# Feature products of q as 64x32 tiles, and output stores placed behind feature moves, in a fused attention and feed-forward kernel

## The chip, the core and the metric

The kernel runs on one NeuronCore of a Trainium2 chip. The core has a matrix engine (TensorE, "PE" in the profile, its weight loads "PEld"), a vector engine (VectorE, DVE), a scalar engine (ScalarE, ACT), a general engine (GpSimd, POOL) and a queue that issues transfers (SyncE, SP). They run side by side and wait for each other through semaphores. The metric is the device time of one execution in microseconds; the lower the better.

## The reference

Inputs are q, k and v of 4 batches, 4 heads, 1088 positions and 32 channels, two sketch matrices S1 and S2 of 8x32, and the two weight matrices of a feed-forward layer, 128x2048 and 2048x128. All are 32-bit floats.

```python
def phi(x):                       # 64 features of each position
    a = einsum('rd,bhsd->bhsr', S1, x)
    b = einsum('rd,bhsd->bhsr', S2, x)
    return einsum('bhsi,bhsj->bhsij', a, b).reshape(..., 64)
kv  = einsum('bhsf,bhsd->bhfd', phi(k), v)
z   = sum(phi(k), axis=2)
num = einsum('bhsf,bhfd->bhsd', phi(q), kv)
den = einsum('bhsf,bhf->bhs', phi(q), z)[..., None] + 1e-6
x   = (num / den).transpose(0, 2, 1, 3).reshape(4352, 128)
h   = maximum(x @ w_in, 0)
out = (h * h) @ w_out
```

## The kernel before

The feed-forward layer is most of the work. The 4352 rows of x are cut into 12 chunks: 4 batches with 3 chunks each, of 384, 384 and 320 positions. For each chunk the 2048 hidden units are cut into 16 blocks of 128. One block of one chunk is a step, and there are 192 steps, in the list `steps`. In step i TensorE makes the first product of step i+3 (`ffn1`, L908, output `pg`, half-precision operands) and the second product of step i (`ffn2`, L939, output `po`, 32-bit operands, collected over the 16 blocks). In between the relu and the square of `pg` are made by ScalarE, VectorE or GpSimd (L902, L918, L920, L929); `balance()` chooses which.

The attention of later chunks is made in the same steps, a little in each. A planner, `_Plan`, keeps a list of functions for each step. `P.add` puts a function at the first step that lies behind what it needs and where its engine has room, and `P.fix` puts it at a given step. In the end the main loop emits, for each step, the two products and then the functions in that step's list, in the order in which they were put in. Each engine works off its own instructions in the order of emission, and so does the SP queue, which stands still while the transfer at its head waits for its data.

For a chunk of batches 1 to 3 the attention goes through these functions:

- `a_qT` turns q (VectorE), and `a_qgy` (L564) multiplies it with `sw`, which holds the folded sketch matrices. The contraction runs over 64 rows, in two halves r, and the positions of the chunk are two halves of 192 (160 in the last chunk). Its output is the tile `qg`, named `qk` in the profile; half r goes to bank r of it.
- `a_tq` (L573) turns the outcome back, `a_den` makes the denominators, `a_qp2` (GpSimd) the 64 features, and `a_bk` (L612) turns these again, into `ft` and `u1`.
- `a_mv` (L626) moves rows of features between partitions, by transfers on the SP queue: two copies inside `ft` and then four from `u1`, named `u` in the profile, to `ft`. Two of the four overwrite what the first two read, and so they wait for these.
- `a_nd2` (L637) multiplies the features with `kw`, which comes from k and v; its output `ndn` is the attention before scaling. It is a product of 64 rows by 32 columns in eight tiles of the array.

`x_group` emits on TensorE, in this order: `a_nd2` of one chunk, `a_qgy` of the next chunk, and, where a new batch is due, `a_kf2` (L431), the features of k, again as 64 by 32 tiles. In batch 0 `a_ndn` (L550) stands in the place of `a_nd2`, with the same tile shape. One group has `a_qgy` alone, the first of batch 1. A matmul of 32-bit floats shows as two instructions in the trace.

The output of a chunk is scaled (`f_sc`, L985), turned (`f_sT`, L994, tile `oT` of two buffers) and stored by four transfers on the SP queue (`out_dma`, L1010). For chunk m these stand at steps 16(m+1) and 16(m+1)+2. The loads of k, v and q for the next batch (`loads`, L131, L141) are on the same SP queue.

Of the kernel before, what the change touches and what calls it, by code (L numbers as in the profile page):

```python
# [15 lines left out]
def _ap(t: bass.AP, p0: int, np_: int, off: int, free):  # L16

    p = list(t.ap)[0]
    return bass.AP(
        t.tensor, t.offset + p0 * p[0] + off, [[p[0], np_]] + [list(d) for d in free]  # L20
    )
# [52 lines left out]
def kernel(  # L74
# [13 lines left out]
    B, H, S, D = 4, 4, 1088, 32  # L88
# [9 lines left out]
    SP = 128 * NT  # L98
# [140 lines left out]
    st = {}  # L239
# [3 lines left out]
    sw = [cpool.tile([128, 64], F32, name="sw%d" % i) for i in range(2)]  # L243
# [265 lines left out]
    def width(ch):  # L509
        return min(192, (S - 384 * ch) // 2)  # L510
# [46 lines left out]
    def a_qgy(b, ch, qg):  # L557

        n = width(ch)
        st[b, "qg", ch] = qg  # L560
        for r in range(2):
            for g in range(2):
                c0 = 384 * ch + n * g
                nc.tensor.matmul(  # L564
                    qg[64 * g : 64 * g + 64, 512 * r : 512 * r + n],
                    sw[b % 2][64 * r : 64 * r + 64, :],
                    qT[64 * r : 64 * r + 64, c0 : c0 + n],
                )

# [421 lines left out]
    def f_sT(b, ch):  # L991
        n = min(384, S - 384 * ch)
        oT = fpool.tile([128, 384], F32, tag="oT", bufs=2, name="oT")
        nc.vector.transpose(oT[:, 0:n], st["sc", b, ch][:, 0:n])  # L994
        out_dma(b, ch, oT, n)

    def f_ob(b, ch):
        n = min(384, S - 384 * ch)
# [9 lines left out]
    def out_dma(b, ch, ob, n):  # L1008
        for dm in range(4):
            nc.sync.dma_start(  # L1010
                bass.AP(
                    out.tensor, out.offset + (b * S + 12 * ch) * 128 + 32 * dm,
                    [[G * 128, 32], [128, n // 32], [1, 32]],
                ),
                _ap(ob, 32 * dm, 32, 0, [[32, n // 32], [1, 32]]),
            )
# [106 lines left out]
    for h in range(H):  # L1123
        c0 = 12 * (h % 2)
# [38 lines left out]
    P = _Plan(NS + 4, {"PE": 0.95, "DVE": 1.2, "ACT": 0.6, "POOL": 5.0, "SP": 9.0})  # L1163
    for m in range(B * 3 - 1):
        b, ch = divmod(m, 3)
# [26 lines left out]
    def old_chunk():  # L1192

        b, ch = 0, 1
        P.at["qb", b, ch] = -1
        for e in range(E):
            P.add(("qa", b, ch, e), "DVE", 0.58, [("qb", b, ch)], a_qa, b, ch, e)
            P.add(("qp", b, ch, e), "DVE", 0.56, [("qa", b, ch, e)], a_qp, b, ch, e)
        P.add(("nd", b, ch), "PE", 0.9, [("qp", b, ch, 1)], a_nd, b, ch)
        P.add(("x1", b, ch), "DVE", 0.9, [("nd", b, ch)], a_x1, b, ch)  # L1200
        P.add(("x2", b, ch), "DVE", 0.9, [("x1", b, ch)], a_x2, b, ch)
        P.add(("x3", b, ch), "DVE", 0.7, [("x2", b, ch)], a_x3, b, ch)
        P.at["N"] = P.at["x3", b, ch]
        P.add(("xd", b, ch), "SP", 0.0, [("x3", b, ch)], a_xd, b, ch)
        ready(b, ch)

    def feature_tasks(b, ch):
        need = [("qg", b, ch)] if ("qg", b, ch) in P.at else []
        if b == 0:
            for s_ in range(2):  # L1210
                for i in range(2):
                    P.add(("sh", b, ch, s_, i), "DVE", 0.58, need, a_sh, b, ch, s_, i)
                P.add(("qpn", b, ch, s_), "POOL", 0.95, [("sh", b, ch, s_, 1)], a_qpn, b, ch, s_)
            P.at["X"] = P.at["sh", b, ch, 1, 1]
            return
        P.add(("tq", b, ch), "DVE", 0.5, need, a_tq, b, ch)
        P.at["X"] = P.at["tq", b, ch]
        P.add(("den", b, ch), "DVE", 1.1, [("tq", b, ch)], a_den, b, ch, lag=0)
        for e in range(2):
            P.add(("qp2", b, ch, e), "POOL", 1.05, [("den", b, ch)], a_qp2, b, ch, e)  # L1220
        for e in range(2):
            P.add(("bk", b, ch, e), "DVE", 0.5, [("qp2", b, ch, e)], a_bk, b, ch, e)
            P.add(("mv", b, ch, e), "SP", 0.0, [("bk", b, ch, e)], a_mv, b, ch, e)
        P.at["mv", b, ch, 1] += 5

    def run(*todo):
# [17 lines left out]
    def nd_tasks(b, ch):  # L1244

        need = ["N", ("kw", b)]
        need += [("qpn", b, ch, 1)] if b == 0 else [("mv", b, ch, 1)]
        qc, kb = None, None
        time = 0.75 if b == 0 else 0.4
        if b > 0 and (b, ch) != (B - 1, 2):  # L1250
            qc = divmod(3 * b + ch + 1, 3)
            need += ["X", ("qT", *qc), ("sy", qc[0])]
            time += 0.45
        if (b == 0 and ch == 2) or (ch == 0 and 0 < b < B - 1):
            kb = b + 1
            need += ["X"] + [("kT", kb, x_) for x_ in range(3)]
            time += 0.5
        P.add(("nd", b, ch), "PE", time, need, x_group, b, ch, qc, kb)
        if qc:
            P.at["qg", *qc] = P.at["nd", b, ch]  # L1260
        if kb:
            P.at["kf", kb] = P.at["nd", b, ch]

    def x_tasks(b, ch):
        if b == 0:
            P.add(("dT", b, ch), "DVE", 0.58, [("nd", b, ch)], a_dT, b, ch)
            P.add(("rd", b, ch), "DVE", 0.4, [("dT", b, ch)], a_rd, b, ch, lag=0)
            P.add(("rb", b, ch), "DVE", 0.58, [("rd", b, ch)], a_rb, b, ch, lag=0)
            P.add(("x", b, ch), "DVE", 0.56, [("rb", b, ch)], a_x, b, ch, lag=0)
        else:  # L1270
            P.at["x", b, ch] = P.at["nd", b, ch]
        P.add(("ax", b, ch), "ACT", 0.5, [("x", b, ch)], a_ax, b, ch)
        P.add(("sum", b, ch), "PE", 0.17, [("ax", b, ch)], a_sum, b, ch)
        P.add(("rs", b, ch), "DVE", 0.53, [("sum", b, ch)], a_rs, b, ch)
        if b > 0:
            P.add(("xs", b, ch), "DVE", 0.56, [("rs", b, ch)], a_xs, b, ch, lag=0)
        P.add(("s2", b, ch), "DVE", 0.53, [("sum", b, ch)], a_s2, b, ch)
        if b == 0:
            P.add(("xs", b, ch), "POOL", 0.95, [("rs", b, ch)], a_xs, b, ch)
            P.at["N"] = P.at["s2", b, ch]  # L1280
        else:
            P.at["N"] = max(P.at["s2", b, ch], P.at["xs", b, ch])
        P.add(("bt", b, ch), "POOL", 1.0, [("s2", b, ch)], a_beta, b, ch)
        if (b, ch) == (B - 1, 2):
            P.add(("bcol", b, ch), "DVE", 0.5, [("bt", b, ch)], a_bcol, b, ch, lag=3)
        ready(b, ch)
# [14 lines left out]
    def turn_q(n, i):  # L1301
        c0, c1 = 384 * i, min(384 * i + 384, S)
        P.add(("qT", n, i), "DVE", 0.55, [("qg", n, i - 1)] if i else [("qg", n - 1, 2)] if n > 1 else [],
              a_qT, n, c0, c1, first=48 * (n - 1) + 14, slow=1.2)

    def kv_tasks(n):
        P.add(("kv", n), "PE", 1.3, [("kp", n, 0), ("kp", n, 1), "N"], a_kv9, n)
        P.add(("kvs", n), "ACT", 0.3, [("kv", n)], a_kvs, n)
        P.add(("gm", n), "DVE", 0.2, [("kv", n)], a_gm, n)
        P.add(("kvT", n), "PE", 0.3, [("kvs", n), ("gm", n)], a_kvT, n)  # L1310
        P.add(("kw", n), "ACT", 0.3, [("kvT", n)], a_kw, n, lag=1)
        P.add(("sy", n), "DVE", 0.2, [("kvT", n)], a_sy, n, lag=1)
        P.at["N"] = max(P.at["kw", n], P.at["sy", n])

    def turn_k(n):
        s0 = 48 * (n - 1) - (n > 1) * 16
        for i in range(5):
            at = 2 * i if n == 1 else s0 - 16 if i == 0 else s0 + 1 + 2 * i
            P.fix(("ld", n, i), "SP", 0.0, at, loads, n, i)
        for part in range(3):  # L1320
            P.add(("kT", n, part), "DVE", (0.71, 0.71, 0.2)[part], [], a_kT, n, part,
                  first=max(s0, 6), slow=n > 1 and 1.2)

    P.at["X"] = P.at["N"] = -1
    P.add(("kw", 0), "ACT", 0.4, [], a_kw, 0)
    old_chunk()
    f_br(0, 0, 0, 1)
# [18 lines left out]
    for m in range(3, 3 * B):  # L1346
        n, ch = divmod(m, 3)
        if m == 99:
            P.cap["DVE"] = CAP
        if ch == 0 and n + 1 < B:  # L1350
            turn_k(n + 1)
        nd_tasks(n, ch)
        if True:
            x_tasks(n, ch)
        if m + 1 < 3 * B:
            feature_tasks(*divmod(m + 1, 3))
        if False:
            x_tasks(n, ch)
        if ch == 0 and n + 1 < B:
            k_tasks(n + 1)  # L1360
        if ch == 1 and n + 1 < B:
            kv_tasks(n + 1)
        if m + 2 < 3 * B:
            turn_q(*divmod(m + 2, 3))

    def balance():

# [85 lines left out]
```

## Time and profile before

| | |
|---|---|
| median of four runs | 195.74 us (195.16 to 196.02) |
| the profiled execution: its own time | 196.02 us |
| its span in the trace | 194.2 us |
| busy, TensorE matmul | 186.7 us (96%) |
| busy, ScalarE | 130.6 us (67%) |
| busy, VectorE | 118.6 us (61%) |
| busy, GpSimd | 90.5 us (47%) |
| share of 16 DMA engines used by the main queue | 28.7% |
| mean granted clock of TensorE | 0.988 |

The span runs from the first to the last instruction of the traced execution; the execution's own time also holds what lies around it. Busy time of TensorE is modelled to the end of each matmul, and neighbouring matmuls overlap, so a group's cost is read from its start to the start of what follows. "64*32" in a row is the shape of the tile in the array, rows by columns, and "64x192" the operand that streams through it.

### The profile page before, as it was taken

The numbers are of one execution on the slowest core, as the hardware profiler recorded it, in microseconds if no ns is written. First come the engines' busy times: TensorE is split into PE (matmuls) and PEld (weight loads), VectorE is DVE, ScalarE is ACT, GpSimd is POOL, SyncE is SP. The second block draws the span as 40 slices with busy tenths as digits, with TensorE's granted clock in tenths as the row PEclk, the third lists the DMA queues.
The fourth block names the chain that finished last, engine by engine and source line by source line (L and its number), as shares of the span: only waits on it lengthen the run. The fifth ranks groups of instructions, "written<-read, shape, count | busy, mean of one in ns | idle before, by whom it ended". The sixth has DMA issues, their size and how long they took to land.

```text
span 194.2 us, 4289 instructions
## 1 busy us (share of the span) xinstructions
PE 186.7 (96%) x1468; PEld 109.3 (56%) x1468; DVE 118.6 (61%) x284; ACT 130.6 (67%) x322; POOL 90.5 (47%) x172
## 2 busy tenths in 40 slices
PE   7997999999999999999999999999999999999990
PEld 2663565565546546655556556555565555556990
DVE  3958875975639946367339855585381834637750
ACT  3325676956949958678659776577594966856840
POOL 5835553783444944325646941533666542251000
PEclk9999699999999999999999999999999999999998
DMA  5699307020045420341146211022032030200201
GB/s 175 161 318 291 75 7 248 0 33 11 22 86 126 150 46 17 66 128 32 34 87 182 70 29 41 13 42 51 10 56 51 3 66 17 40 4 0 44 0 34
DMA packets 30080, 13.91 MB, mean 72 GB/s; under 512 B 20202, under 2 KB 28778, under 8 KB 30058
## 3 DMA queue, kind: packets, MB, share of 16 engines
q1 hardware_dynamic: 29910, 13.58, 28.7%
q8 instruction: 11, 0.18, 0.4%
q14 instruction: 11, 0.09, 0.2%
q10 hardware_dynamic: 148, 0.07, 0.1%
HBM read 8.80 MB, written 2.23 MB: 57 GB/s over the span
## 4 chain that ended last, share of the span: by engine, by line
PE 85%; DVE 4%; POOL 3%; issue 2%; SPq 2%; ACT 1%; DMA 1%; ACTq 0%; POOLq 0%
PE po L939 52%; PE pg L908 15%; PE kvp L393 3%; PE ndn L637 2%; PE warm L1060 2%; PE qk L564 2%; PE pt L956 2%; SPq L141 2%; PE nd L778 2%; POOL kp L361 2%; POOL g L929 1%; PE rep L1084 1%; ACT gt L918 1%; DVE kp L361 1%; DMA vn<-in_v_dram 1%
## 5 line engine op out<-in xcount | busy, mean ns | idle before, releaser
L939 PE MATMUL po<-g,w_o 128*128 128x384 f32 (+3 forms) x386 | 145.3, 463 | 0.0
L918 ACT ACTIVATE gt<-pg 128x384 f32<-128x384 f32 (+2 forms) x139 | 65.2, 472 | 37.1 <-PE pg L908 36.5
L939 PEld LDWEIGHTS po<-g,w_o 128*128 128x128 f32 x386 | 66.3, 192 | 33.5 <-ACT g L902 15.4
L902 ACT ACTIVATE g<-gt 128x384 f32<-128x384 f32 (+1 forms) x146 | 72.1, 505 | 7.0 <-DVE gt L920 6.5
L908 PE MATMUL pg<-xT,w_in 128*128 128x384 f16 (+2 forms) x193 | 61.5, 320 | 0.7 <-ACT xT L880 0.3
L929 POOL TENSOR_TENSOR g<-gt 128x384 f32<-128x384 f32 (+1 forms) x44 | 34.8, 799 | 47.4 <-ACT gt L918 47.3
L920 DVE TENSOR_SCALAR gt<-pg 128x384 f32<-128x384 f32 (+1 forms) x54 | 28.8, 534 | 27.4 <-PE pg L908 20.0
L908 PEld LDWEIGHTS <-w_in 128*128 128x128 f16 x193 | 19.2, 100 | 22.4 <-issue 5.0
L599 POOL TENSOR_TENSOR qp<-tq,bs 128x384 f32<-128x384 f32 (+1 forms) x18 | 14.2, 811 | 16.9 <-DVE bs L591 16.9
L361 POOL TENSOR_TENSOR kp<-fs 128x384 f32<-128x384 f32 x9 | 13.2, 1492 | 1.3 <-DVE fs L352 1.3
L573 DVE STREAM_TRANSPOSE tq<-qk 128x384 f32<-128x384 f32 (+1 forms) x9 | 5.0, 561 | 13.1 <-PE qk L564 8.0
L738 POOL TENSOR_TENSOR bt<-s 128x384 f32<-128x384 f32 (+1 forms) x10 | 8.2, 816 | 7.1 <-DVE s L712 7.1
L971 POOL COPY br<-beta 32x3 f32<-32x3 f32 x32 | 5.8, 182 | 6.3 <-DVE beta L861 5.1
L985 DVE SCALAR_TENSOR_TENSOR sc<-po,bt 128x384 f32<-128x384 f32 (+1 forms) x9 | 4.8, 531 | 6.4 <-PE po L939 6.3
L361 DVE TENSOR_TENSOR kp<-fs 128x1152 f32<-128x1152 f32 x3 | 7.3, 2430 | 0.0
L720 DVE TENSOR_SCALAR rs<-ndn 128x384 uint32<-128x384 uint32 (+1 forms) x9 | 4.8, 536 | 3.7 <-PE ndn L704 3.5
L393 PEld LDWEIGHTS kvp<-kp,vn 128*32 128x32 f32 x288 | 5.4, 110 | 2.7 <-issue 1.1
L1060 PE MATMUL warm<-zero 128*128 128x512 f16 x16 | 5.7, 521 | 1.2 <-DVE zero L169 1.2
L393 PE MATMUL kvp<-kp,vn 128*32 128x64 f32 x288 | 6.5, 223 | 0.0
L325 DVE STREAM_TRANSPOSE qT<-qn 128x384 f32<-128x384 f32 (+1 forms) x12 | 6.4, 536 | 0.0
L637 PE MATMUL ndn<-ft,kw 64*32 64x192 f32 (+1 forms) x144 | 5.7, 325 | 0.0
L956 PE MATMUL pt<-w_o,g 128*128 128x128 f32 x32 | 5.7, 274 | 0.0
(147 smaller groups left out, 155.2 us busy)
## 6 DMA issues: line engine op xcount, KB each, us to landing
vn<-in_v_dram SPq DMA_DIRECT2D x32, 64.0 KB, 2.0
kn<-in_k_dram SPq DMA_DIRECT2D x3, 544.0 KB, 4.8
qn<-in_q_dram SPq DMA_DIRECT2D x3, 544.0 KB, 4.1
ft<-u SPq DMA_DIRECT2D x24, 48.0 KB, 1.9
out_dram<-oT SPq DMA_DIRECT2D x24, 48.0 KB, 1.9
w_in<-in_moe_w_in_dram SPq DMA_DIRECT2D x2, 512.0 KB, 7.1
w_o<-in_moe_w_out_dram SPq DMA_DIRECT2D x2, 512.0 KB, 8.4
ft<-ft SPq DMA_DIRECT2D x12, 48.0 KB, 1.8
```

The source lines that it names most:

```text
L361: (nc.vector if g == 0 else nc.gpsimd).tensor_tensor(out=_ap(st[b, "kp2"], 0, 128, 128 * (NT * g + lo), [[64, 2 * (hi - lo)], [8, 8], [1, ...
L393: nc.tensor.matmul(st[b, "kvp"][32 * h : 32 * h + 32, 0:64], _ap(vn[b], 0, n, v0 + dv * h, [[1, 32]]), kp[0:n, at[h] : at[h] + 64], start= ...
L599: nc.gpsimd.tensor_tensor(out=_ap(qp, 0, 128, 0, [[32, m], [8, 4], [1, 8]]), in0=_ap(st[b, "tq", ch], 0, 128, 4 * e, [[32, m], [1, 4], [0, ...
L637: nc.tensor.matmul(nd[32 * h : 32 * h + 32, 512 * g : 512 * g + n], st[b, "kw"][64 * g : 64 * g + 64, 32 * h : 32 * h + 32], st[b, ch, "ft ...
L902: nc.scalar.activation(dst, src, Square)
L908: nc.tensor.matmul(pg[:, c0:c1], w_in[:, 128 * c : 128 * c + 128], st[b, "xT"][:, 384 * ch + c0 : 384 * ch + c1],)
L918: nc.scalar.activation(gt[:, c0:c1], pg[:, c0:c1], Relu)
L920: nc.vector.tensor_scalar(out=gt[:, c0:c1], in0=pg[:, c0:c1], scalar1=0.0, scalar2=None, op0=amax)
L929: (nc.vector if on[1] == "DVE" else nc.gpsimd).tensor_tensor(out=g2[:, c0:c1], in0=gt[:, c0:c1], in1=gt[:, c0:c1], op=mult)
L939: nc.tensor.matmul(st["po", b, ch][:, c0:c1], w_o[:, 128 * c : 128 * c + 128], g2s[i][1][:, c0:c1], start=first, stop=(c == NFF - 1), skip ...
L956: nc.tensor.matmul(st["pt"][:, 0:128], g2s[i][1][:, 0:128], w_o[:, 128 * c : 128 * c + 128], start=(c == 0), stop=(c == NFF - 1),)
L1060: nc.tensor.matmul(t_[:, 0:512], zero[:, 0:128], zero[:, :])
```

## The change

In `a_qgy` each 64-column product becomes two 32-column products: the output rows are written in four blocks of 32 instead of two of 64, and each matmul reads 32 of the 64 columns of `sw`. What is computed is the same.

`f_sT` no longer issues the store of its chunk; a new function `f_st` does. A list `moves` holds the step of the last `a_mv` of each chunk. The store of chunk m, for m from 2 to 10, is put at step 16(m+1)+2, or, where an entry of `moves` lies in that step or the nine behind it, at the last such entry. As it is put in after everything else, it is emitted last in its step.

```diff
@@ def a_qgy(b, ch, qg):
         for r in range(2):
-            for g in range(2):
-                c0 = 384 * ch + n * g
+            for o in range(4):
+                c0 = 384 * ch + n * (o // 2)
                 nc.tensor.matmul(
-                    qg[64 * g : 64 * g + 64, 512 * r : 512 * r + n],
-                    sw[b % 2][64 * r : 64 * r + 64, :],
+                    qg[32 * o : 32 * o + 32, 512 * r : 512 * r + n],
+                    sw[b % 2][64 * r : 64 * r + 64, 32 * (o % 2) : 32 * (o % 2) + 32],
                     qT[64 * r : 64 * r + 64, c0 : c0 + n],
                 )
@@ def f_sT(b, ch):
         nc.vector.transpose(oT[:, 0:n], st["sc", b, ch][:, 0:n])
-        out_dma(b, ch, oT, n)
+        st["oT", b, ch] = oT
+
+    def f_st(b, ch):
+        out_dma(b, ch, st["oT", b, ch], min(384, S - 384 * ch))
@@ def feature_tasks(b, ch):
             P.add(("mv", b, ch, e), "SP", 0.0, [("bk", b, ch, e)], a_mv, b, ch, e)
+        moves.append(P.at["mv", b, ch, 1])
         P.at["mv", b, ch, 1] += 5
@@
     P.at["X"] = P.at["N"] = -1
+    moves = []
     P.add(("kw", 0), "ACT", 0.4, [], a_kw, 0)
@@
             turn_q(*divmod(m + 2, 3))
 
+    for m in range(2, B * 3 - 1):
+        s_ = 16 * (m + 1) + 2
+        s_ = max([s_] + [x_ for x_ in moves if s_ <= x_ < s_ + 10])
+        P.fix(("st", m), "SP", 0.0, s_, f_st, *divmod(m, 3))
+
     def balance():
```

## The prediction

> **What bounds the kernel now.** I read the page's busy shares and its chain that ended last first, then the waits, then TensorE's timeline around the steps that the change touches, and last the SP queue's timeline.
>
> ```profile
> span 194.2 us, 4289 instructions
> PE 186.7 (96%) x1468; PEld 109.3 (56%) x1468; DVE 118.6 (61%) x284; ACT 130.6 (67%) x322; POOL 90.5 (47%) x172
> PE 85%; DVE 4%; POOL 3%; issue 2%; SPq 2%; ACT 1%; DMA 1%; ACTq 0%; POOLq 0%
> ```
>
> The second line is busy time by engine, the third the chain's shares. TensorE is busy 96% of the span and is 85% of the chain. By stretches, it was busy 135.88 of the 136 us between 42 and 178 us, and there two matmul lines alternate at a fixed pitch: a 128x384 step starts every 0.81 us, of which the second product is 0.65 us (two instructions) and the first 0.16 us. So between 42 and 178 us TensorE's own time is the time, but for the short stalls counted below. What is taken out of TensorE's stream there comes off the end.
>
> The next two stretches are TensorE's timeline: start, length, instruction, count. A row's length includes a modelled tail, so a group's cost is its start to the next group's start.
>
> ```profile
> 30.96 0.78 PE L550 MATMUL ndn<-qp,kw 64*32 64x160 f32 x32
> 31.53 0.69 PE L431 MATMUL qk<-kq,sk 64*32 64x288 f32 x16
> 32.16 0.34 PE L908 MATMUL pg<-xT,w_in 128*128 128x384 f16 x1
> ...
> 56.64 0.56 PE L637 MATMUL ndn<-ft,kw 64*32 64x192 f32 x16
> 57.12 0.56 PE L564 MATMUL qk<-qT,sw 64*64 64x192 f32 x8
> 57.61 0.71 PE L431 MATMUL qk<-kq,sk 64*32 64x288 f32 x16
> 58.26 0.31 PE L908 MATMUL pg<-xT,w_in 128*128 128x320 f16 x1
> ```
>
> ```profile
> 138.32 0.56 PE L637 MATMUL ndn<-ft,kw 64*32 64x192 f32 x16
> 138.81 0.56 PE L564 MATMUL qk<-qT,sw 64*64 64x192 f32 x8
> 139.30 0.31 PE L908 MATMUL pg<-xT,w_in 128*128 128x320 f16 x1
> ```
>
> Look at where the tile shape (64*32, 64*64) changes between neighbours. 384 columns by two instructions stream in 0.65 us, so 192 columns stream in 0.325, 160 in 0.27, 288 in 0.485. In the batch 1 to 3 groups L637 costs 0.48 to 0.49, L564 0.49, L431 0.65: each is its stream plus 0.165. In the batch 0 group (first stretch) two groups of one shape stand side by side. L550 has two matmuls for each of the eight 64x32 tiles, so its stream is 0.54; with L431's 0.485 that is 1.025, and both together took 1.20 (30.96 to 32.16). They paid about 0.175 once, where two groups apart would pay 0.33. A change of tile shape costs some 0.155.
>
> **The change: the products.** a_qgy (L564) runs in nine groups. Each has 4 matmuls, 8 instructions in the trace; with 32 output columns each, it has 8 matmuls, 16 instructions. Streams per tile are the same: the four 64x64 tiles hold one matmul each, the eight 64x32 tiles one each. The nearest row for the new group alone is L637, also 16 instructions of 64*32 with 192 columns: 0.48 to 0.49, as L564 now (0.43 against 0.43 at 160 columns). So alone it costs nothing more. That holds for the one group that stands alone (46.56 us).
>
> In the other eight, L637 stands directly ahead, already 64*32. There the shape change goes: 8 x 0.155. In two of them (56.64 and 99.36 us) L431 follows, also 64*32, and a second one goes: 2 x 0.155. Sum: 10 x 0.155 = 1.55 us less TensorE time. After the eight groups 128x128 products follow as before, so that change stays.
>
> Here the Trainium skill has a rule that speaks against the change. In "TensorEngine Tiling (Array Packing)", section Instruction Overhead, each matmul has about 60 cycles of overhead, and one should not tile a dimension that is already small. At the 2.4 GHz of "TensorE: Matmul & The Clock Gate" that is 25 ns, an estimate: 8 more instructions in 9 groups would be 72 x 25 ns = 1.8 us more, and the kernel 0.3 us slower even with the shape changes gone. The trace decides: L550 started 32 instructions in 0.57 us (17.8 ns each, their weight loads included), almost exactly its stream, so the overhead lay beside other tiles' streams. Bounds for a group of two: 17.8 ns x 32 = 0.57 is under the stream of 0.65 and costs nothing; 25 ns x 32 = 0.80 would eat the whole 0.155. I take the row.
>
> Downstream, tq (L573, VectorE) waits for the products and gets them no later. The vector, scalar and move work that must be done by the next group starts at the end of this group, so nearly all of it moves forward with TensorE. Not all. Where TensorE already waited:
> - 69.00 us: L637's second half waited for the moves ft<-u; the group took 1.46 instead of 0.92, 0.54 late. The moves' first part lay behind the q load (issued at 61.65 us, about 4.1 us to landing), and that load is issued by an SP queue that has run without pause since 56.92 us. This is clock time that doesn't move forward when the group at 56.64 gets 0.31 shorter. I take 0.3 us back here.
> - 109.07 us: 0.24 behind VectorE's gt, whose row of work begins after the group at 99.36 ends; it moves along. Nothing.
> - 149.03 us: 0.25 behind moves whose source was ready at 143.87 (VectorE, after the group at 138.32); it moves along. Nothing.
>
> **The change: the stores.** The planner's arithmetic puts the second row of moves of the chunks at steps 31, 45, 59, 73, 92, 106, 120, 134 and 148. Stores of chunks 2 to 10 stand at steps 50, 66, 82, ... 178; a store goes to the last move in its next ten steps. Six go later (50 to 59, 66 to 73, 98 to 106, 114 to 120, 130 to 134, 146 to 148); those at 82, 162 and 178 stay, so the kernel's tail is untouched. Each is 4 DMA issues, 1.9 us of SP's time, passed by 6 move issues (3.6 us), and in the first case the store stands ahead of the next k load.
>
> ```profile
> 141.69 1.88 SPq L1010 DMA_DIRECT2D out_dram<-oT  x4
> 143.93 1.33 SPq L626 DMA_DIRECT2D ft<-ft  x2
> 145.36 2.44 SPq L626 DMA_DIRECT2D ft<-u  x4
> 154.46 1.99 SPq L1010 DMA_DIRECT2D out_dram<-oT  x4
> 156.55 1.14 SPq L626 DMA_DIRECT2D ft<-ft  x2
> 157.80 2.43 SPq L626 DMA_DIRECT2D ft<-u  x4
> ```
>
> SP waited 43.6 us for oT at the stores and 26.0 us for ft at the moves: it is idle before both, and what is moved costs SP nothing that is missed. Did a store hold up a move? Only once: ft of the last case was ready at 155.28, the moves began at 156.55, behind the store's end at 156.45, 1.2 us late. They land by 162.0, and the group at 161.56 took 0.50 where another of its size took 0.43. That 0.07 can be won. At 141.69 the store ended at 143.57, before ft was ready (143.87); in the other four it ended 3 us or more ahead. What a later store could hold up: the buffer oT has two, and the turn two chunks on needs the store landed. The tightest is 12 us off (store issued to 82.2, next turn near 96). The k load at 80.36 goes to 82.2 and is read at step 80, near 95. With that cover gone, VectorE would wait for the part of 1.9 us that is uncovered. Stores now issued behind the moves could slow their landing; that is shown nowhere. Bound: at most 1 us at 149.03, the only place without margin that has a store behind its moves, and at best the 0.25 there is won. I take 0: the store is issued after the moves, and its packets come behind theirs.
>
> **Sum.** -1.55 + 0.3 - 0.07 = -1.3 us against the profiled execution's own 196.02 (194.2 span and 1.8 around it), so 194.7. The median of the four runs is 195.74, 0.28 lower: 194.4.
>
> **The rivals.** (1) The waits take it over. If what TensorE gains is lost at each place where it waited already, the 0.31 of the first group goes at 69.00, the 0.155, 0.155 and 0.31 of the next three at 109.07, the next three 0.155 at 149.03; left are 0.155 and 0.07, 195.5. For it: stalls there show no slack. Against it: the late chains start from the end of the groups that get shorter. (2) Slower: issue decides. TensorE would have to start 32 pairs of load and product in each group, and if such a pair costs more than 26 ns there (the 0.82 us of a merged group by 32), the group is issue bound and the gain turns round; at the rule's 25 ns for each of the 72 added instructions with no shape change saved, +1.8 us, 197.5. For it: TensorE's trace shows only one run of 32, with other operands. Against it: that run took 17.8 ns. (3) The shape change isn't what the 0.165 is, and a semaphore wait between L637 and L564 stays: no gain but the 0.07, 195.7. Against it: L564 shows no wait on another engine but one of 0.3 us.
>
> **How the numbers follow.** The likeliest case, 0.7: 193.9 to 195.1 (the 1.55 whole, with 0.25 more from stalls, to half of it). Rival 1: 0.13, rival 3: 0.07, rival 2: 0.1. The range goes from 193.8 to 195.8 and takes in rivals 1 and 3. What a measurement of this kernel can tell from no change is about 0.3%, 0.6 us. Faster by more: most of the likeliest case and a part of rival 1, 0.74; within: 0.15; slower: 0.11.
>
> **What would show it.** In the changed profile L564 has 144 instructions of 64*32. L637 to the next L908 should take 0.82 to 0.84 (192 columns) where it was 0.98, and the triples 1.31 where they were 1.62. The group at 69 should wait some 0.8 instead of 0.54 for ft<-u. Six stores should follow their moves in the SP queue, the last moves starting near 155.3 less what was gained. I am wrong if the groups still take 0.98 or more, or if TensorE's pitch of 0.81 opens right behind them.

## The result and the profile after

The changed kernel took 194.67 us (median of 43 runs, 193.28 to 198.24), the kernel before 196.01 us (64 runs). The ratio is 0.9933 with a 95% interval of 0.9914 to 0.9951: 1.3 us, 0.7% faster. A second series gave 0.9955 (0.9929 to 0.998), 0.9 us; the two intervals overlap. The ratios leave out the few executions of a kernel that took over 1.5% longer than its fastest.

The head of the profile after: span, busy time by engine, shares of the chain.

```profile
span 191.6 us, 4421 instructions
PE 183.7 (96%) x1540; PEld 109.4 (57%) x1540; DVE 118.4 (62%) x284; ACT 130.4 (68%) x322; POOL 90.6 (47%) x172
PE 81%; DVE 5%; SPq 5%; DMA 3%; issue 2%; ACT 1%; DVEq 0%; ACTq 0%
```

TensorE has 72 more matmul instructions and yet 3.0 us less busy time, a part of it by the clock (below). In the chain SPq has 5% where it had 2%, and DMA 3% where it had 1%: somewhere TensorE now waits for transfers. The two spans differ by 2.6 us, and that is not the change alone. The first group that both kernels have in common (L550) starts at 30.96 us before and at 29.14 us after, so 1.82 us were already there. The next rows, before and then after, are the same stretch of 4 us; the number behind the POOL column is the granted clock.

```profile
18.00:22.00 4.00, 4.00 (x27) 2.29 (x27) 3.70 (x10) 2.70 (x7) 2.62 (x11) 0.64 0.63 138
```

```profile
18.00:22.00 4.00, 4.00 (x32) 2.09 (x31) 3.71 (x12) 3.45 (x9) 2.35 (x10) 1.00 0.64 152
```

The traced execution of before had 0.64 of the clock there, the other had all of it: 0.36 of 4 us is 1.4 of the 1.82 us, an estimate. The code of that stretch is the same in both. What the change did is read from the first group to the end: 163.24 us before, 162.46 us after, 0.78 us less. In a second execution of each it is 163.45 and 162.99, 0.46 us less. Both are under the timed 1.3 us; the rest is in no line of these traces.

Now the groups. TensorE's timeline after, at the triple group and at the pair near 109 us:

```profile
54.81 0.56 PE L637 MATMUL ndn<-ft,kw 64*32 64x192 f32 x16
55.16 0.53 PE L564 MATMUL qk<-qT,sw 64*32 64x192 f32 x16
55.48 0.69 PE L431 MATMUL qk<-kq,sk 64*32 64x288 f32 x16
56.11 0.31 PE L908 MATMUL pg<-xT,w_in 128*128 128x320 f16 x1
...
109.21 1.00 PE L637 MATMUL ndn<-ft,kw 64*32 64x192 f32 x12
109.87 0.34 PE L564 MATMUL qk<-qT,sw 64*32 64x160 f32 x4
...
110.57 0.34 PE L908 MATMUL pg<-xT,w_in 128*128 128x384 f16 x1
```

The triple takes 1.30 us from its start to L908 where it took 1.62: three groups side by side in one tile shape. The pair near 109 us shows L637 drawn out over 1.00 us, with only 12 of its instructions in the first row: it stands still in its middle. The group that stands alone (L564 without L637, first of batch 1) shows that the halved products save nothing by themselves. It takes 0.49 us up to L908 in both kernels, before and then after:

```profile
46.56 0.56 PE L564 MATMUL qk<-qT,sw 64*64 64x192 f32 x8
47.05 0.34 PE L908 MATMUL pg<-xT,w_in 128*128 128x384 f16 x1
```

```profile
44.73 0.56 PE L564 MATMUL qk<-qT,sw 64*32 64x192 f32 x16
45.22 0.34 PE L908 MATMUL pg<-xT,w_in 128*128 128x384 f16 x1
```

This table has the other nine places, each from the start of L637 to the start of L908, for the kernel before and after and for kernels of the next section, by chunk (batch, chunk of the batch); in (3,2) L637 stands alone. The two rows "again" are second executions of the same two kernels.

| us | 1,0 | 1,1 | 1,2 | 2,0 | 2,1 | 2,2 | 3,0 | 3,1 | 3,2 | sum |
|---|---|---|---|---|---|---|---|---|---|---|
| before | 1.62 | 1.46 | 0.92 | 1.62 | 0.92 | 0.92 | 0.98 | 1.17 | 0.50 | 10.11 |
| before again | 1.62 | 1.35 | 0.92 | 1.62 | 0.93 | 0.92 | 0.98 | 1.53 | 0.44 | 10.31 |
| after | 1.30 | 1.55 | 0.76 | 1.30 | 1.36 | 0.76 | 0.81 | 0.83 | 0.44 | 9.11 |
| after again | 1.30 | 1.61 | 0.76 | 1.30 | 1.36 | 0.76 | 0.81 | 0.82 | 0.44 | 9.16 |
| products alone | 1.30 | 1.78 | 0.75 | 1.30 | 1.36 | 0.76 | 1.04 | 0.82 | 0.49 | 9.60 |
| stores alone | 1.62 | 1.36 | 0.92 | 1.62 | 0.93 | 0.92 | 0.98 | 1.46 | 0.44 | 10.25 |
| q load later | 1.30 | 0.76 | 0.76 | 1.29 | 1.17 | 0.76 | 0.81 | 0.82 | 0.43 | 8.10 |
| loads moved | 1.30 | 0.76 | 0.76 | 1.30 | 1.01 | 0.76 | 0.87 | 0.83 | 0.43 | 8.02 |
| before, shifted | 1.62 | 1.58 | 0.92 | 1.62 | 0.92 | 0.92 | 0.97 | 0.98 | 0.43 | 9.96 |
| after, shifted | 1.30 | 1.77 | 0.76 | 1.30 | 1.22 | 0.76 | 0.81 | 0.82 | 0.43 | 9.17 |
| loads moved, shifted | 1.30 | 0.75 | 0.76 | 1.30 | 0.77 | 0.76 | 0.81 | 0.82 | 0.43 | 7.70 |
| the same, early stores | 1.30 | 0.76 | 0.76 | 1.30 | 0.76 | 0.76 | 0.81 | 0.81 | 0.43 | 7.69 |

Each group without a wait got 0.16 to 0.17 shorter, the triples 0.32. Three groups carry waits, and they changed in three ways: (1,1) waits longer, (2,1) waits and didn't before, (3,1) waits 0.07 (0.83 against 0.76) where it waited 0.25. The sum is 1.00 us less. Of that, 0.16 goes back ahead of (2,1): from the end of (2,0) to its start it is 10.60 us before and 10.76 after. A wait of L637's first product lies ahead of the group and isn't in the table. There are three more of these: 0.67 us ahead of (2,1) in "after again", and ahead of (1,1) 0.63 in "products alone" and 0.21 in "after, shifted". The trace's waits of L637 say what for, in after and then, for 99 to 111 us, in after again:

```profile
  PE pg L908: 4.7, 9
  DMA ft<-u: 1.0, 3
```

```profile
PE ndn L637 <- DMA ft<-u: 0.6, 1, 0.6
```

Before, the row for ft<-u was 0.3 us, once. The stall that before has at 109.07 us, behind VectorE, is as long after; before and then after:

```profile
107.98 0.33 PE L908 MATMUL pg<-xT,w_in 128*128 128x384 f16 x1
109.07 0.32 PE L908 MATMUL pg<-xT,w_in 128*128 128x384 f16 x1
```

```profile
105.45 0.33 PE L908 MATMUL pg<-xT,w_in 128*128 128x384 f16 x1
106.54 0.32 PE L908 MATMUL pg<-xT,w_in 128*128 128x384 f16 x1
```

### The profile page after: what moved, and what is told of

It reads as the page before. It is cut to its first block, busy times and chain, and to the rows that moved or that the text cites. A ratio compares the mean times of both kernels' runs of the same rounds, so it can differ in the third digit from the quotient of the medians.

```text
span 191.6 us, 4421 instructions
## 1 busy us (share of the span) xinstructions
PE 183.7 (96%) x1540; PEld 109.4 (57%) x1540; DVE 118.4 (62%) x284; ACT 130.4 (68%) x322; POOL 90.6 (47%) x172
## 4 chain that ended last, share of the span: by engine, by line
PE 81%; DVE 5%; SPq 5%; DMA 3%; issue 2%; ACT 1%; DVEq 0%; ACTq 0%
PE po L939 50%; PE pg L908 14%; PE kvp L393 3%; PE ndn L637 2%; SPq L141 2%; PE warm L1063 2%; PE pt L956 2%; DMA ft<-ft 2%; PE nd L778 2%; PE qk L564 1%; PE rep L1087 1%; SPq L626 1%; SPq L1013 1%; DMA ft<-u 1%; DVE kp L361 1%
## 5 line engine op out<-in xcount | busy, mean ns | idle before, releaser
L908 PE MATMUL pg<-xT,w_in 128*128 128x384 f16 (+2 forms) x193 | 61.0, 317 | 0.7 <-ACT xT L880 0.3
L908 PEld LDWEIGHTS <-w_in 128*128 128x128 f16 x193 | 19.1, 99 | 22.0 <-issue 4.3
L637 PE MATMUL ndn<-ft,kw 64*32 64x192 f32 (+1 forms) x144 | 6.1, 325 | 0.3 <-DMA ft<-u 0.2
```

What stands on the lines that cost most here:

```text
L637: nc.tensor.matmul(nd[32 * h : 32 * h + 32, 512 * g : 512 * g + n], st[b, "kw"][64 * g : 64 * g + 64, 32 * h : 32 * h + 32], st[b, ch, "ft ...
L908: nc.tensor.matmul(pg[:, c0:c1], w_in[:, 128 * c : 128 * c + 128], st[b, "xT"][:, 384 * ch + c0 : 384 * ch + c1],)
```

## The experiments

**One change at a time.** The first edit is the products alone, the second the stores alone.

```diff
 # products alone: a_qgy as in the changed kernel, f_sT as before
 # stores alone: f_st and its steps as in the changed kernel, and
-            for o in range(4):
-                c0 = 384 * ch + n * (o // 2)
+            for g in range(2):
+                c0 = 384 * ch + n * g
...
```

> The q products as 64x32 tiles alone, stores where they were. Theory A (the gain is TensorE's shape changes, the stores do nothing): the groups take what they take with both changes: pairs 0.76 from L637 to L908, the two triples 1.30, waits of some 0.8 us at the group near 67 us and 0.4 to 0.6 at the group near 109 us, and a time 0.993 of before. Theory B (part of the gain is the later stores): the group near 147 us waits 0.2 to 0.3 again as before (1.0 instead of 0.83), the last one takes 0.50 instead of 0.44, and the time is 0.994 to 0.996.

> The later stores alone, products as before. Theory A: pairs stay at 0.98 and 0.92, the triples at 1.62, nothing is won but at most 0.07 us at the last group: 0.999 to 1.001 of before. Theory B: the group near 149 us loses its wait of 0.25 and the last group its 0.07: 0.998 (0.3 us). A loss from stores in the way of moves would show as longer groups near 149 us.

Measured: products alone 0.9943 (0.992 to 0.9967), stores alone 0.9946 (0.992 to 0.9972), and the changed kernel beside them:

> The changed kernel itself, on the chip of this call, for comparison: 0.993 of before, a wait of 0.8 us at the group near 67 us and of 0.4 to 0.6 at the one near 109 us, if these are not an accident of one execution.

It gave 0.9955 (0.9929 to 0.998). The table shows the products alone with every shortening that both changes together have, and with the waits at (1,1) and (2,1) too; with the 0.63 ahead of it, (1,1) lost 1.65 us, twice what was expected, and the trace has 163.43 us from the first group to the end, no gain over before. (3,1) lost its wait without the later stores, against theory B; the last group's 0.49 would be for it. Here (3,0) waited 0.23, which no other kernel shows in that size.

The stores alone are the odd one. Theory A said 0.999 to 1.001, and the interval lies below that. Its profile has nothing to show for it: the groups sum to 10.25, between the two executions of before, (3,1) waits 0.54, and the last group's 0.44 is also what before takes in its second execution. The kernel before against itself came out at one:

> The kernel before against itself, for the size of what chance makes: 1.000 with an interval that holds 1. If it comes out near 0.995 too, the 0.9946 of the stores alone is chance, and its profile (groups unchanged or longer) is to be believed. Its group near 69 us should wait 0.3 to 0.6 us and the one near 111 us not at all.

1.0013 (0.9983 to 1.0043). This is another series, and no offset of half a per cent shows in it. The stores' ratio stays unexplained by any line of its profile: from the first group to the end it has 163.39 us, between the two executions of before. One more pair of kernels bears on it, at the end.

**Is it the tile shape?** One matmul of eight columns was put between L637 and L564 in the eight groups, on the whole array in one kernel and as a 64x32 tile in the other.

```diff
+        if qc and b > 0:
+            # one kernel has this line (other shape):
+            nc.tensor.matmul(t_[:, 480:488], zero[:, 0:128], zero[:, 0:8])
+            # the other kernel this one (same shape):
+            nc.tensor.matmul(t_[0:32, 480:488], zero[0:64, 0:32], zero[0:64, 0:8])
         if qc:
             a_qgy(*qc, t_)
```

> Both changes, and in each of the eight groups one half-precision matmul of eight columns on the full 128x128 array between L637 and L564, so that the tile shape changes twice again; it multiplies zeros into columns that nothing reads. Theory A (a change of tile shape is what costs): each group gets 0.25 to 0.4 us longer than with the matmul in the same shape, the pairs some 1.1, and the time is at least 2 us over the kernel with the same-shape matmul. Rival (the 0.15 saved belongs to the fewer output columns or to the order of the banks): groups stay within 0.05 us of those with the same-shape matmul.

> Both changes, and the same extra matmul of eight columns as a 64x32 tile, so that the tile shape stays. Both theories: some 0.02 to 0.06 us a group over the changed kernel; pairs 0.78 to 0.82, triples 1.32 to 1.36, and the time within 0.5 us of the changed kernel's.

TensorE's timeline at the pair (1,2), first with the other shape, then with the same:

```profile
82.77 0.50 PE L637 MATMUL ndn<-ft,kw 64*32 64x160 f32 x16
83.21 0.18 PE L1244 MATMUL qk<-zero 128*128 128x8 f16 x1
83.32 0.56 PE L564 MATMUL qk<-qT,sw 64*32 64x192 f32 x16
83.81 0.34 PE L908 MATMUL pg<-xT,w_in 128*128 128x384 f16 x1
```

```profile
82.29 0.50 PE L637 MATMUL ndn<-ft,kw 64*32 64x160 f32 x16
82.58 0.17 PE L1244 MATMUL qk<-zero 64*32 64x8 f16 x1
82.59 0.52 PE L564 MATMUL qk<-qT,sw 64*32 64x192 f32 x16
83.05 0.34 PE L908 MATMUL pg<-xT,w_in 128*128 128x384 f16 x1
```

The same tiny product, and the group takes 1.04 us or 0.76. In the first, L564 starts 0.55 after L637, in the second 0.30. Two changes of shape cost 0.28 us here, 0.27 and 0.28 in the other groups without a wait. The weights that the tiny product loads also differ (128x128 and 64x32), but their load took 96 and 93 ns. In the same shape the tiny product is free, below what was expected. Times: 1.0019 (0.9993 to 1.0045) against 0.9917 (0.9883 to 0.9951), 2.0 us apart where eight groups by 0.28 make 2.2. The shape change is the cost; order, banks and the number of columns that stream are the same in both.

**Is the q load what the moves wait for?** One line moves the load of q for the next batch behind the moves.

```diff
-            at = 2 * i if n == 1 else s0 - 16 if i == 0 else s0 + 1 + 2 * i
+            at = 2 * i if n == 1 else s0 - 16 if i == 0 else s0 + 14 if i == 4 else s0 + 1 + 2 * i
```

> Both changes, and the q load of the next batch put behind the moves of its time (step 46 instead of 41, and 94 instead of 89). Theory A says that the waits of 0.79 us at the group near 67 us and some 0.6 at the one near 109 us come from moves queued behind that load, which didn't move forward with TensorE: both groups fall to 0.76, and the time to 0.987 of before (1.2 us less than with both changes). Rival: the moves are late by their own pace (the last two wait for the first two), then both waits stay within 0.2 us and the time at 0.993.

At (1,1) the wait is gone, 1.61 to 0.76, as theory A said. At (2,1) 0.41 is left of the 0.76 of after (0.16 ahead of the group, 0.60 in it). The time is 0.9866 (0.9826 to 0.9905), 0.9% under the changed kernel in the same series.

The q load is needed for the wait at (1,1). What made the wait longer is another thing, that the SP queue's rows show, before and then after:

```profile
56.92 3.73 SPq L141 DMA_DIRECT2D vn<-in_v_dram  x8
62.85 1.15 SPq L626 DMA_DIRECT2D ft<-ft  x2
```

```profile
55.11 4.59 SPq L141 DMA_DIRECT2D vn<-in_v_dram  x8
61.23 1.15 SPq L626 DMA_DIRECT2D ft<-ft  x2
```

Before, the queue was through with the q load at 62.08 us and then idle until the features were ready at 62.85, 4.59 us behind the end of the group ahead (58.26). So there was slack. After, one of the eight v load issues took 1.28 us instead of 0.43, and the moves began 5.12 us behind that group (56.11). In the five executions with a triple of 1.30 us and the q load in its old place, the whole wait at (1,1) follows the length of that one issue: 0.62 us for an issue of 1.21, 0.79 for 1.28, 0.86 for 1.31, 1.22 for 1.51 and 1.65 for 1.92. In the kernel with the other shape the q load came 0.81 us later behind the group than in before, within the slack, and the wait was 0.44 (1.48 where the same group without a wait takes 1.04), no longer than before. What lengthens such an issue comes under theory C.

The second edit moved the v loads ahead as well (steps 33 and 75):

> Both changes, the q load behind the moves (steps 46 and 94) and the v loads ahead of the store and moves (step 33 for batch 2, step 75 for batch 3). Theory A: the moves ahead of the groups near 69 and 111 us then find empty queues, both groups take 0.76, no other group waits, and the time is 0.983 to 0.986 of before, up to 0.4 us under the kernel with the q load alone moved. Rival: what is left at 111 us (0.41) comes from two moves that wait for two others, whatever stands before them, and stays.

0.9861 (0.9819 to 0.9903); (2,1) is at 1.01, a wait of 0.25, and (3,0) waits 0.06. Theory A, empty queues and no wait, had now failed twice at (2,1). Nothing is loaded there any more when the moves begin, and the SP queue still spends 3.52 us on four issues:

```profile
104.16 1.62 SPq L626 DMA_DIRECT2D ft<-u  x1
105.83 0.59 SPq L626 DMA_DIRECT2D ft<-u  x1
106.52 0.53 SPq L626 DMA_DIRECT2D ft<-u  x1
107.15 0.54 SPq L626 DMA_DIRECT2D ft<-u  x1
```

One issue takes 1.62 us instead of 0.54, and the rival (they wait for each other) doesn't account for that. The changed kernel has the same at the same place, here from its SP timeline, and the instruction queue in that stretch (104.8 to 106.2 us):

```profile
104.33 0.54 SPq L626 DMA_DIRECT2D ft<-u  x1
104.91 1.61 SPq L626 DMA_DIRECT2D ft<-u  x1
107.25 0.51 SPq L626 DMA_DIRECT2D ft<-u  x1
```

```profile
q8 instruction: 1, 0.02, 5.7%
```

A packet of queue q8, instructions, is under way. In the kernel before, a long issue stands in the moves of (1,2) instead, again with such a packet (77.8 to 79.4 us), and another packet lies in the moves of (3,1), the group that waited before (143.8 to 145.0 us). These are, one after the other, the long issue, its packet, and the packet at (3,1):

```profile
77.94 1.74 SPq L626 DMA_DIRECT2D ft<-u  x1
```

```profile
q8 instruction: 1, 0.02, 5.4%
```

```profile
q8 instruction: 1, 0.02, 4.7%
```

**Theory C: TensorE's instruction fetches.** The page counts 11 such packets before and 12 after, 0.18 and 0.20 MB, so 16 KB each. Counting TensorE's matmuls and weight loads up to each packet in the trace, they are some 250 apart in the mean, with single steps from 101 to 372. Seven of the nine packets from the third on come within 5 of the same count in both kernels (one at 1980 and 1979, another at 2490 and 2485), the other two 43 and 85 later after. The change puts 16 more instructions into each group (8 weight loads, 8 products), so the same count comes earlier: the first of these packets came at 112.6 us before, after the group (2,1), and comes at 104.9 us after, in the middle of its moves; the second came at 144.0 us, in the moves of (3,1), and comes at 133.3 us, in a store. The Trainium skill has the same block: "Runtime: NRT & Kernel Launch", section Instruction fetch mechanics, says that an engine's instructions are refilled in 16 KiB blocks of 256, and calls the cost mostly hidden. For TensorE it is hidden here too: across the packet at 83.53 us of the changed kernel its steps keep their pitch, 0.81 us from 83.27 to 84.08. For SP it isn't. The v load of 1.28 us ahead of (1,1) after has such a packet under way as well (56.95 us); before, none lies there.

This can be tried without touching anything near the groups: more instructions at the very start shift all later fetches.

```diff
-    keep_warm(WARM0)
+    for _ in range(32):
+        nc.tensor.matmul(st["warm"][:, 0:128], zero[:, 0:128], zero[:, 0:128])
```

> The kernel before, with its first nine 512-column warm-up products of zeros as 32 products of 128 columns: 46 more TensorE instructions at the very start, nothing else. Theory C (TensorE's instruction fetches come at fixed counts of its instructions, about every 256, and a transfer issue of SP that meets one takes up to 1.2 us longer): the fetch that met the moves near 144 us in before comes near 139 us instead, and the wait of 0.25 to 0.6 us at the group near 149 us goes (group 0.92); the one at 77.9 us stays within the moves there, which have time. Time 0.997 to 0.999 of before. Rival (the slow issues belong to the load of the transfer engines, or to stores ahead of the moves): the wait at that group stays.

> Both changes, with the same 46 more instructions at the start. Theory C: the fetch that met the moves near 105 us comes near 100, and the group near 109 us takes 0.76 to 0.95 instead of 1.36 (some of it may be the q load ahead of the moves); the group near 67 us still waits some 0.8 for the q load; all others as before. Time 0.989 to 0.992 of before. Rival (the q load alone makes the wait near 109 us): that group stays at 1.36.

> Both changes, loads moved, and the 46 more instructions. Theory C: the last wait, 0.25 us at the group near 109 us, goes; all eight groups take 0.76 to 0.83 (triples 1.30). Time 0.983 to 0.986 of before, 0.2 to 0.3 us under the one with the loads moved alone. Rival: 1.01 stays at that group.

The group (3,1) of the kernel before, from its second execution and then with the shift:

```profile
147.80 1.17 PE L637 MATMUL ndn<-ft,kw 64*32 64x192 f32 x16
148.90 0.50 PE L564 MATMUL qk<-qT,sw 64*64 64x160 f32 x8
149.33 0.34 PE L908 MATMUL pg<-xT,w_in 128*128 128x384 f16 x1
```

```profile
147.81 0.61 PE L637 MATMUL ndn<-ft,kw 64*32 64x192 f32 x16
148.35 0.50 PE L564 MATMUL qk<-qT,sw 64*64 64x160 f32 x8
148.79 0.34 PE L908 MATMUL pg<-xT,w_in 128*128 128x384 f16 x1
```

It starts at the same moment and takes 0.98 instead of 1.53, where 0.92 is its size without a wait. The packet came at 138.24 us instead of 143.09, at a count of 2494 instead of 2492. In this stretch of the SP queue, the two ft<-ft issues took 1.70 us and 1.15 us:

```profile
142.70 1.70 SPq L626 DMA_DIRECT2D ft<-ft  x2
```

```profile
142.70 1.15 SPq L626 DMA_DIRECT2D ft<-ft  x2
143.95 2.43 SPq L626 DMA_DIRECT2D ft<-u  x4
```

With the loads moved, (2,1) falls from 1.01 to 0.77, as theory C said. In the changed kernel with the shift it falls only from 1.36 to 1.22, short of the 0.76 to 0.95 expected: the fetch now meets a v load ahead of the q load (1.48 us for one issue), and the q load still stands ahead of the moves. At (1,1) it waits longer than expected, 1.22 us with the 0.21 ahead, as the v load there took 1.51. In all fourteen traces of this study every issue of SP over 1 us between 38 and 186 us has a q8 packet under way. The reverse doesn't hold: before has a packet at 62.4 us that leaves the issues at 0.52 and 0.59.

The times: before shifted 0.9959 (0.9927 to 0.9991), after shifted 0.9964 (0.9934 to 0.9993) where 0.989 to 0.992 was expected, loads moved and shifted 0.9854 (0.9798 to 0.9911). In the profiled executions of the last two the granted clock was low at the start: from 15 to 25 us 0.69 and 0.63 after shifted, 0.74 and 0.92 with the loads moved too. Their first groups came at 36.41 and 34.48 us. Whether the other warm-up products bring this about isn't shown; before shifted, with the same ones, had 1.00 there. The shift is a probe, not an improvement, and the groups are its result.

**Without the later stores.** The last kernel has the products, the loads moved and the shift, with the stores at their steps of before.

> The same without the later stores: products as 64x32 tiles, loads moved, 46 more instructions, stores at their steps of before. Theory A (the stores do nothing where nothing else disturbs the moves): groups as with the later stores, but the last one at 0.44 to 0.50; times of the two within 0.15%. Theory B (later stores are worth something): this one is 0.2% or more slower, and one of the groups near 67, 109 or 147 us shows a wait for ft<-u.

Its groups are those with the later stores to 0.01 us each; no group's L637 is shown waiting for ft<-u. The group near 109 us:

```profile
108.29 0.56 PE L637 MATMUL ndn<-ft,kw 64*32 64x192 f32 x16
108.64 0.48 PE L564 MATMUL qk<-qT,sw 64*32 64x160 f32 x16
109.05 0.34 PE L908 MATMUL pg<-xT,w_in 128*128 128x384 f16 x1
```

0.9802 (0.9743 to 0.9862) against 0.9854 (0.9798 to 0.9911): if anything faster without the later stores, with intervals that overlap. The expected 0.15% between the two can't be read from ratios this wide; the traces have 160.82 us from the first group to the end in both. The two ratios are the lowest of this study. In this pair theory B has no group to stand on.

## Why the prediction was right, point by point

The forecast was 1.3 us less; it was 1.3 us (0.67%). The total came out better than its terms.

- *Ten shape changes, 1.55 us.* Right in mechanism and size: six groups by 0.16 to 0.17 and two triples by 0.32 make 1.6 us in the table, and the tiny product put two changes back for 0.28. The rule that spoke against it, the Trainium skill's 60 cycles for each matmul ("TensorEngine Tiling (Array Packing)", section Instruction Overhead), does not add up to a cost here: L637 and L564 together start 32 products in 0.67 us (54.81 to 55.48), which is their stream, and a further tiny product was free.
- *0.3 us back at (1,1), because the q load doesn't move forward with TensorE.* Right in place and near in size: the wait grew from 0.54 to 0.79, in the second executions from 0.43 to 0.86, and it went when the load was put behind the moves. The reason given is not what the runs show. The moves had slack behind the q load, and they came later because a v load issue ahead met an instruction packet; the wait follows the length of that issue. No run here has the short triple without that packet, so what would be lost then isn't measured. That 0.3 came out is in part luck.
- *Nothing back at 109.07 us, since VectorE's row moves along.* Right: from one L908 to the next it is 1.09 us in both. What went wrong is the silent step behind it, that no new wait comes at (2,1). There 0.76 us are lost, 0.16 ahead of the group and 0.60 in it, and 1.27 in the second execution. The prediction counted the added instructions' time, and not that they shift the points at which TensorE fetches its program, nor that an SP issue that meets a fetch takes 1.6 us (2.0 in the second execution). The loads ahead add to it: with the loads moved away and an issue of 1.62 us, 0.25 was left. How much of it is the q load's own isn't shown, as with that load alone moved the long issue took 1.21.
- *(3,1) keeps its 0.25.* Wrong, the other way: the same shift took the fetch out of its moves, and 0.18 (0.55 in the second execution) was won.
- *0.07 for the last store.* Not shown: the last group takes 0.44 in the second execution of before too, and 0.43 in the last kernel, with the stores early. No group of these profiles is shorter by the later stores alone beyond what two executions differ by. That the stores alone were timed at 0.9946 is left open.
- *The sum.* As measured in the first pair of traces the terms are -1.60, +0.25, +0.76, -0.18 and -0.06, together -0.83 us, and from the first group to the end the traces have -0.78. The second pair has -0.46. The timed 1.3 us is more than that, and 1.3 was forecast without the wait at (2,1). The hit is in part luck, and where the remaining half microsecond comes from is open.
- The rivals: the waits took over a part, at one place that rival 1 named (69.00) and at one that it did not (2,1). Rival 2 (issue decides) and rival 3 (a wait stays between the groups) are out by the triple at 1.30.

## What to carry to other kernels

Order TensorE's work so that tiles of one shape stand side by side, and give a small product its neighbour's tile shape, even at twice the instructions: each change of shape was 0.14 to 0.16 us here. When one engine gets faster, check the margin of each wait behind it, and what stands ahead of the awaited transfer in its queue; moving the q and v loads won about as much again as the change. TensorE instructions added ahead moved later fetches in every kernel here that had them, so a wait that appears or goes far from an edit can be theirs: look at the instruction queue in that stretch before looking for a cause in the code.

## What the runs showed of the hardware

An instruction fetch of TensorE (one 16 KB packet on its own queue) held up many of the SP queue's issues that met it: 1.0 to 2.0 us, where a move takes 0.5 to 0.6. Such a packet was under way in every issue over 1 us between 38 and 186 us of fourteen traces, but not every packet lengthened the issue it met. By what path it does so isn't shown. The place follows TensorE's instruction count: it was the same within a few instructions in a second execution (2490 and 2492) and with the stores alone moved (2492), and came earlier in time with products added ahead.
